# Two more feed-forward tiles beside the attention, and the last unit's reciprocals spread over rows by the matmul engine

## The chip, the cores and the metric

The kernel runs on one core of a Trainium2 chip. The metric is the device time of one execution in microseconds (us). Engines are named as in the profile: PE (matmul), DVE (vector), ACT (scalar), POOL (GpSimd), SP (sync, which issues most transfers).

## The reference

One transformer block with modulation, for 2048 tokens of width 512 in fp32 (F is 1792):

```
mod = silu(c) @ w_mod                            # six vectors of 512: sa, ca, ga, sb, cb, gb
h = layernorm(x) * (1 + ca) + sa
q, k, v = h @ wqkv                               # 32 heads of 16
x = x + ga * (softmax(q k^T / 4) v) @ wo
h = layernorm(x) * (1 + cb) + sb
x = x + gb * ((silu(h @ w_gate) * (h @ w_up)) @ w_down)
```

## The kernel before

**Layout.** The 2048 queries are cut into four chunks of 512 (`NC`, `CW`). Four heads of one chunk are a **unit**; there are 8 x 4 = 32 units (`NU`), and each has 16 **steps**, one for each 128 keys, so 512 steps (`n`) in all. A step is four **pairs**, one for each head. A pair (`pair_of`, L961) is a score matmul (L568) with its exponential on ACT (L570), and beside it on other rows of the array a matmul (L521) that finds, 20 steps ahead, the maxima of a later unit, reduced by DVE (L523). After step 491 no maxima are left. The product with V (`pv_step`, L574, matmuls at L583) follows at least two steps behind. The exponentials are L570, four to a step (one of 128 x 512 for each head), so the number of L570 instructions up to a moment, divided by four, is the step that has been reached.

**Sums of the softmax.** V carries a column of ones, so row 16 of each head's 32 rows in the result `o` is the sum of its exponentials. When a unit ends, `out_a` to `out_c` (L590 to L611) move the four sums (4 x 512 numbers) to a 128 x 16 tile `dn`, take reciprocals (L598), store them to DRAM (L599), load them again with every head's row repeated 32 times (L604), multiply (L610) and store the result to DRAM (`o_dr`, L611). `load_o` (L721) gathers it from there, 16 of each 32 rows, for the output projection; `split_o` (L726) splits it into a high and a low part (L729, L730).

**Precision.** Most products are three matmuls of split operands (high x high, high x low, low x high) in a single-pass format; the array takes fp32 operands in several records.

**Filler.** While units of chunk 1 to 3 run, the output projection and feed-forward of the chunk before stand between their pairs. `plain(steps)` (L1018) runs steps without filler; `filled(places, work)` (L1032) runs two steps (eight pairs) and takes after each pair as many items of `work` as the table `TWO`, `DOWN` or, once no maxima are left, `ALONE` (L50 to L52) says. Filler matmuls use 64 rows of the array at a time (L781), two banks (`FBANKS`, 3 and 6). One gate-and-up tile (`gate_up`, 128 of the 1792 columns) fills four steps; a down job fills two. The 28 jobs of a chunk are in `Chunk.jobs` (L694).

**The order around the change.** For chunk 2, whose feed-forward stands beside the last units: plain to step 403, the projection to step 411, 9 plain steps (`NORM`), 3 with transposes, then `REST` = 24 plain steps to step 447, then all jobs but the last `KEEP` = 7 to step 511, and one step without filler (L1080). The seven jobs left (gate-up tiles 11 and 12, the two downs of pair 5, tile 13, the two downs of pair 6) are run by `whole` (L1086) after the attention with matmuls of 128 rows (L791).

**The end.** After the last product with V (L1101), PE runs in program order: 36 projection matmuls of the last chunk for k = 0 to 2 (`out_terms`, L824), 48 matmuls of tiles 11 and 12 (L1114), 12 projection matmuls for k = 3, which need the last unit's output, then 48 matmuls of the downs and tile 13 (L1123), the transposes of the new rows (L765) and the last chunk's feed-forward. Meanwhile `out_b`, `out_r`, `out_c`, `load_o` and `split_o` of the last unit are issued from ACT (L1109 to L1113).

Of the kernel before, what the change touches and what calls it, by code (L numbers as in the profile page):

```python
# [9 lines left out]
F32 = mybir.dt.float32  # L10
# [9 lines left out]
P = 128  # L20
# [3 lines left out]
DH = 16  # L24
F = 1792
NT = S // P
NK = D // P
NC = 4
CW = S // NC
NG = H // 4  # L30
NU = NG * NC
# [11 lines left out]
UG = 16 * NG  # L43
PTS = 13
FBANKS = (3, 6)
KEEP = 7
REST = 24
NORM = 9
STARTS = (147, 275, 403)
TWO = (0, 3, 2, 2, 2, 2, 1, 0)  # L50
# [4 lines left out]
def run(it):  # L55
    for _ in it:
        pass


def take(it, k):  # L60
    run(islice(it, k))
# [40 lines left out]
def block_kernel(ctx, tc, x, wqkv, wo, w_gate, w_up, w_down, c, w_mod, out):  # L102
    nc = tc.nc
# [8 lines left out]
    banks = [ps.tile([P, CW], F32, name=f"bank{i}") for i in range(8)]  # L112
# [11 lines left out]
    ident = const.tile([P, P], F32, name="ident")  # L124
# [11 lines left out]
    o_dr = dram.tile([NC, NG, P, CW], F32, name="o_dr")  # L136
# [355 lines left out]
    pf = None  # L492
    qop, mx, pts, pv, o_, due, res = {}, {}, {}, {}, {}, {}, {}
    posts = []
    n = 16 * NU
    last = NC - 1
# [75 lines left out]
    def pv_step(i, half):  # L572

        u, kt = divmod(i, 16)  # L574
        g = u % NG
        cols = slice(half * HQ, (half + 1) * HQ)
        if kt == 0 and half == 0:
            pv[u] = single("pv")
            o_[u] = pf.tile([P, CW], F32, name="o", tag="o", bufs=2)
        p_ = pts.pop(i) if half else pts[i]  # L580
        for h in range(4):
            e0 = (kt * H + 4 * g + h) * (DH + 1)
            nc.tensor.matmul(pv[u][32 * h:32 * h + 32, cols], v_flat[:, e0:e0 + 32], p_[h][:, cols],  # L583
                             start=(kt == 0 and half == 0), stop=(kt == 15),
                             skip_group_check=half == 1)
        if kt == 15 and half:
            nc.scalar.copy(o_[u], pv[u])
# [9 lines left out]
    def out_b(u, eng, o, dn):  # L597
        nc.vector.reciprocal(dn, dn)  # L598
        eng.dma_start(d_dr[u].rearrange("h (b e) -> (h b) e", e=16), dn)  # L599
        return o,  # L600

    def out_r(u, eng, o):
        rb = pf.tile([P, CW], F32, name="rb", tag="rb", bufs=1)
        eng.dma_start(rb, d_dr[u][:, None, :].to_broadcast([4, 32, CW]))  # L604
        return o, rb

    def out_c(u, eng, mul, o, rb):
        ci, g = divmod(u, NG)
        on = pf.tile([P, CW], F32, name="on", tag="on", bufs=1)
        mul.tensor_mul(on, o, rb)  # L610
        eng.dma_start(o_dr[ci, g], on)  # L611

    def at(i, f):
        due.setdefault(i, []).append(f)
# [16 lines left out]
    def tmp(name):  # L631
        return pf.tile([P, CW], F32, name=name, tag="tmp", bufs=4)
# [56 lines left out]
    class Chunk:  # L689
# [31 lines left out]
        def load_o(self, eng, ks=range(NK)):  # L721
            for k in ks:
                src = o_dr[self.ci, 2 * k:2 * k + 2].rearrange("g (h e) s -> (g h) e s", e=32)[:, 0:DH, :]
                eng.dma_start(self.oT[1][:, k, :].bitcast(F32), src)

        def split_o(self, ks=range(NK), alone=False):  # L726
            for k in ks:
                hi, lo = self.oT[0][:, k, :], self.oT[1][:, k, :]
                (nc.scalar.copy if alone else nc.gpsimd.tensor_copy)(hi, lo.bitcast(F32))  # L729
                (nc.vector if alone else nc.gpsimd).tensor_sub(lo, lo.bitcast(F32), hi.bitcast(F32))  # L730
# [90 lines left out]
    def out_terms(ch, t, pt, ks):  # L821
        for k in ks:
            for a, b in ((0, 0), (0, 1), (1, 0)):
                nc.tensor.matmul(pt, ch.oT[a][:, k, t * P:(t + 1) * P], ch.wo[k // 2][:, b, k % 2, :],  # L824
                                 start=(k == 0 and a == b == 0), stop=(k == NK - 1 and a == 1))
# [46 lines left out]
    chunks = {}  # L872
# [21 lines left out]
    def hook():  # L894
        while posts:
            posts.pop(0)()
# [64 lines left out]
    def pair_of():  # L961
        nonlocal done
        i = done // 4 - 1
        most = 4 * n - 4 * (LEAD - 1)
        h = (ORDER if done < most else (0, 1, 2, 3))[done % 4]
        work = [lambda: score(i + 1, h)]
        if done < most:
            work.insert(1 - h % 2, lambda: max_one(done + 4 * (LEAD - 1)))
        for f in work:
            f()  # L970
        done += 1
        if side:
            side.pop(0)()
# [22 lines left out]
    def pvs(most, by_halves):  # L996

        nonlocal owed
        if by_halves:
            most, owed = most + owed, 0  # L1000
        while most and halves and 4 * halves[0][0] + 8 <= done:
            i, half = halves.pop(0)
            pv_step(i, half)
            most -= 1
            if i % 16 == 15 and half:
                close_unit(i // 16, done // 4 - 1)
                if by_halves:
                    break
        if by_halves and most and halves and 4 * halves[0][0] + 8 <= done:
            owed = most  # L1010

    def end_steps():
        nonlocal ended
        while ended < done // 4:
            after(ended - 1)
            ended += 1

    def plain(steps, tails=()):  # L1018

        nonlocal four, bank, beside  # L1020
        beside = False
        assert steps % WIN == 0 and done % 4 == 0
        four, bank = Turn(0, 1, 2, 3), Turn(4, 5, 6)
        for w in range(4 * steps // WIN):
            for _ in range(WIN):
                pair_of()
            if w >= 4 * steps // WIN - len(tails):
                tails[w - 4 * steps // WIN](four())
            pvs((HALVES[(w - 2) % 4] if done > 8 else 0) + (w == 4 * steps // WIN - 1), True)
            end_steps()  # L1030

    def filled(places, work):  # L1032

        nonlocal four, bank, beside
        beside = True
        four, bank = three, Turn(4, 5)
        if done >= 4 * n - 4 * (LEAD - 1):
            places, bank = ALONE.get(places, places), Turn(4, 5, 0, 1, 2)
        for r in range(len(places)):
            pair_of()  # L1040
            take(work, places[r])
            if r % 4 == 3:
                end_steps()
        hook()
        pvs(6, False)
# [9 lines left out]
    at(n - 24, begin_last)  # L1055
    at(n - 13, lambda: chunks[last].load_o(nc.gpsimd, range(NK - 1)))
    at(n - 11, lambda: chunks[last].split_o(range(NK - 1)))
    outs = [banks[b] for b in FBANKS]
    pvs(3, False)
    for ci in range(last):  # L1060
        plain(STARTS[ci] - done // 4)
        ch = chunks[ci]
# [7 lines left out]
        if ci == last - 1:  # L1070
            plain(REST)
        for _ in range(len(ch.jobs) - (KEEP if ci == last - 1 else 0)):
            job, args = ch.jobs.pop(0)
# [3 lines left out]
            for places in (TWO, TWO) if job is gate_up else (DOWN,):  # L1077
                filled(places, work)
    chunks[last - 1].load_gu(NF - 2)
    filled((0,) * 4, iter(()))  # L1080


    assert done == 4 * n
    turns = chain([2, 3, 2, 0, 1, 2, 0], cycle([1, 3, 2, 0]))

    def whole(ch, jobs):  # L1086
        for job, args in jobs[:-2]:
            b = 2 * next(turns)
            for _ in job(ch, *args, banks[b:b + 2], False):
                yield  # L1090
            hook()
        both = []
        for job, args in jobs[-2:]:
            b = 2 * next(turns)
            both.append(job(ch, *args, banks[b:b + 2], False))
        for g in both * 2:
            yield from islice(g, 6)
            hook()

    for i, half in halves:  # L1100
        pv_step(i, half)  # L1101
    after(n - 1)
    close_unit(NU - 1, n)
    ch, chp = chunks[last], chunks[last - 1]
    rest = whole(chp, chp.jobs)
    ch.load_x2(nc.gpsimd)
    for t in range(4):
        out_terms(ch, t, banks[t], range(NK - 1))
    on = out_b(NU - 1, nc.scalar, *res[NU - 1])  # L1109
    on = out_r(NU - 1, nc.scalar, *on)  # L1110
    out_c(NU - 1, nc.scalar, nc.vector, *on)
    ch.load_o(nc.scalar, (NK - 1,))
    ch.split_o((NK - 1,), True)  # L1113
    take(rest, 48)  # L1114
    for t in range(4):
        out_terms(ch, t, banks[t], (NK - 1,))
        if t % 2:
# [41 lines left out]
```

## Time and profile before

| what | value |
|---|---|
| median of 3 runs | 1838.07 us (1837.73 to 1839.37) |
| the profiled execution | 1838.88 us |
| its span, first to last instruction | 1837.1 us |
| PE busy | 1825.5 us, 99% of the span |
| DVE, ACT, POOL busy | 1532.5, 1243.7, 460.4 us |
| granted PE clock | 1.00 throughout |

Each row of a timeline gives a start, a duration, the engine, the line, the operation, what it writes and reads, and in brackets how long the engine had been idle and what ended that. A row of windows gives, for a stretch of the span, each engine's busy time and in parentheses how many instructions reach into it. "SPq", "ACTq" and "POOLq" are instructions that only issue a transfer. PE matmuls overlap: a matmul of 512 columns is shown as about 0.39 us and the next one starts some 0.23 us after it, so a PE that is shown as busy may still be waiting a little.

### The profile page before, as it was taken

What the parts mean: (1) busy time and instruction counts of PE and PEld (TensorE: products, weight loads), DVE (VectorE), ACT (ScalarE), POOL (GpSimd) and SP (SyncE); (2) the same over time, 40 slices, a digit from 0 to 9 for tenths busy, and PEclk for the clock granted to TensorE, in tenths of its full rate; (3) what the DMA queues carried; (4) which work ended last, traced back from release to release, by engine and by line L of the source; (5) the groups of instructions that cost most, each with busy time, mean ns of one, the idle gap of its engine ahead of it and who ended that gap; (6) DMA issues with size and microseconds to landing.
All of it is one profiled execution on the core that took longest, in us unless ns stands there. A gap on an engine that the chain in (4) does not pass through costs nothing.

```text
span 1837.1 us, 41048 instructions
## 1 busy us (share of the span) xinstructions
PE 1825.5 (99%) x16904; PEld 1198.2 (65%) x16904; DVE 1532.5 (83%) x2578; ACT 1243.7 (68%) x2386; POOL 460.4 (25%) x541
## 2 busy tenths in 40 slices
PE   9999999999999999999999999999999999999999
PEld 7876444444455777776565777776564577777887
DVE  5578999999999888889999888889999988831544
ACT  4223888888877777777878777777878877774211
POOL 3612544565223111111123111111123011130200
PEclk9999999999999999999999999999999999999999
DMA  8884876657845444453544554444643545333642
GB/s 305 286 225 149 183 185 199 168 189 178 209 79 125 102 120 141 118 147 70 149 103 105 134 132 116 123 117 90 158 81 57 111 93 149 138 122 121 271 169 110
DMA packets 80488, 267.63 MB, mean 146 GB/s; under 512 B 19604, under 2 KB 24212, under 8 KB 59620
## 3 DMA queue, kind: packets, MB, share of 16 engines
q1 hardware_dynamic: 61324, 179.71, 33.8%
q0 software_dynamic: 18288, 84.49, 19.3%
q8 instruction: 133, 2.18, 0.5%
q10 hardware_dynamic: 688, 0.80, 0.2%
q14 instruction: 55, 0.45, 0.1%
HBM read 201.85 MB, written 62.13 MB: 144 GB/s over the span
## 4 chain that ended last, share of the span: by engine, by line
PE 96%; DVE 2%; ACT 1%; DMA 1%; SPq 0%; issue 0%; DVEq 0%
PE bank L583 27%; PE bank L781 19%; PE bank L568 18%; PE bank L521 14%; PE bank L791 8%; PE bank L211 7%; DVE mx L523 1%; PE bank L824 1%; DMA wm_ab<-in_w_mod 1%; PE bank L765 0%; DVE stt L807 0%; PE bank L533 0%; PE bank L163 0%; PE bank L534 0%; PE bank L535 0%
## 5 line engine op out<-in xcount | busy, mean ns | idle before, releaser
L523 DVE TENSOR_REDUCE mx<-bank 128x1 f32<-128x512 f32 x2048 | 1276.0, 681 | 108.5 <-PE bank L521 66.2
L568 PE MATMUL bank<-qop,kop 50*128 50x512 f32 x2048 | 730.2, 425 | 1.0 <-ACT pt__16517 L570 0.2
L521 PE MATMUL bank<-kop,qop 48*128 48x512 f32 x2048 | 726.6, 425 | 2.9 <-DVE mx L523 2.6
L568 PEld LDWEIGHTS bank<-qop,kop 50*128 50x128 f32 x2048 | 342.6, 184 | 169.9 <-issue 55.6
L521 PEld LDWEIGHTS bank<-kop,qop 48*128 48x128 f32 x2048 | 343.5, 184 | 113.9 <-DVE mx L523 67.7
L781 PE MATMUL bank<-act,wgu 64*128 64x512 f32 x1872 | 300.9, 392 | 0.0
L781 PEld LDWEIGHTS bank<-act,wgu 64*128 64x128 f32 x1872 | 196.1, 187 | 24.7 <-issue 0.2
L610 POOL TENSOR_TENSOR on<-o,rb 128x512 f32<-128x512 f32 x31 | 39.8, 1284 | 498.1 <-DMA rb<-d_dr 363.6
L781 PE MATMUL bank<-wd,mid 64*128 64x512 f32 x912 | 134.0, 397 | 0.0
L843 POOL CAST mid<-m 128x512 fp32r<-128x512 f32 x40 | 24.3, 608 | 379.3 <-DVE m L841 176.5
L781 PEld LDWEIGHTS bank<-wd,mid 64*128 64x128 f32 x912 | 88.0, 185 | 15.9 <-ACT first L878 3.2
L211 PE MATMUL bank<-hT,wqs 128*128 128x512 f32 x384 | 94.3, 397 | 0.4 <-DVE wqs L351 0.4
L839 DVE SCALAR_TENSOR_TENSOR q<-th,bank 128x512 f32<-128x512 f32 x56 | 38.2, 682 | 54.4 <-ACT th L835 54.4
L211 PEld LDWEIGHTS bank<-hT,wqs 128*128 128x128 f32 x384 | 70.7, 188 | 18.8 <-issue 2.9
L835 ACT ACTIVATE th<-bank 128x512 f32<-128x512 f32 x56 | 33.3, 594 | 58.1 <-PE bank L791 58.1
L855 DVE TENSOR_TENSOR x<-bank,x 128x512 f32<-128x512 f32 x84 | 53.9, 685 | 18.3 <-PE bank L781 16.8
L841 DVE TENSOR_TENSOR m<-bank,q 128x512 f32<-128x512 f32 x56 | 38.7, 691 | 21.7 <-PE bank L791 19.7
L844 POOL TENSOR_TENSOR mid<-m,mid 128x512 fp32r<-128x512 f32 x40 | 51.5, 1287 | 3.3
L791 PE MATMUL bank<-wd,mid 128*128 128x512 f32 x216 | 51.4, 393 | 0.0
L211 PE MATMUL bank<-wqs,hT 128*128 128x512 f32 x192 | 48.0, 398 | 0.0
L781 PE MATMUL bank<-wgu,act 64*128 64x512 f32 x288 | 47.8, 394 | 0.1
L791 PEld LDWEIGHTS bank<-wd,mid 128*128 128x128 f32 x216 | 40.3, 188 | 9.1 <-POOL mid L844 0.3
(6298 smaller groups left out, 5133.0 us busy)
## 6 DMA issues: line engine op xcount, KB each, us to landing
wgu<-gu_dr SPq DMA_DIRECT2D x48, 1024.0 KB
wd<-wd_dr SPq DMA_DIRECT2D x28, 1024.0 KB
kop<-kd SPq DMA_DIRECT2D x33, 768.0 KB
kop<-kd POOLq DMA_DIRECT2D x29, 768.0 KB, 8.8
gu_dr<-wgu POOLq DMA_DIRECT2D x14, 1024.0 KB, 13.5
kd<-prt SPq DMA_DIRECT2D x16, 512.0 KB
qd<-prt SPq DMA_DIRECT2D x16, 512.0 KB
kop<-gu_dr SPq DMA_DIRECT2D x8, 1024.0 KB
```

Of the source, the lines that this page charges most:

```text
L211: nc.tensor.matmul(pt, lhs(a, k), rhs(b, k), start=(n == 0), stop=(n == 3 * nk - 1))
L521: nc.tensor.matmul(pm, qop[u][rows, s, qt * P:(qt + 1) * P], kop[u % 3][rows, s, kc * CW:(kc + 1) * CW], start=True, stop=True)
L523: nc.vector.tensor_reduce(mx[u][:, b, s, qt, kc:kc + 1], pm, op=ALU.max, axis=AX.X)
L568: nc.tensor.matmul(sp, kop[u % 3][rows, h // 2, kt * P:(kt + 1) * P], qop[u][rows, h // 2, :], start=True, stop=True)
L583: nc.tensor.matmul(pv[u][32 * h:32 * h + 32, cols], v_flat[:, e0:e0 + 32], p_[h][:, cols], start=(kt == 0 and half == 0), stop=(kt == 15), ...
L610: mul.tensor_mul(on, o, rb)
L781: nc.tensor.matmul(outs[e], lhs(e, a, k)[rows], rhs(b, k)[rows], start=(ph == 0 and j == 0), stop=(j == z and (ph == 1 or trade is not None)),
L791: nc.tensor.matmul(outs[e], lhs(e, a, k), rhs(b, k), start=(j == 0), stop=(j == z))
L839: nc.vector.scalar_tensor_tensor(q, th, 1.0, outs[0], op0=ALU.add, op1=ALU.mult)
L841: nc.vector.tensor_mul(m32, outs[1], q)
L844: (nc.gpsimd if slow else nc.vector).tensor_sub(mid[:, 1, :], m32, mid[:, 0, :].bitcast(F32))
L855: nc.vector.tensor_add(ch.x2[:, t, :], outs[e], ch.x2[:, t, :])
```

## The change

- `KEEP` goes from 7 to 5 and `REST` from 24 to 15: tiles 11 and 12 move from behind the attention to its steps 502 to 509; the jobs begin at step 438 instead of 447, and nine plain steps go. The steps without filler at the end become two.
- The two projection loops at the end are cut: 18 matmuls (t = 0, 1) before and 18 (t = 2, 3) behind a new fp32 matmul, and the 48 matmuls of tiles 11 and 12 are no longer there.
- The last unit's reciprocals no longer go through DRAM. DVE multiplies the 128 x 16 reciprocals by a pattern `eye` (one where the row's number within its head is the block's number) into a 128 x 512 tile `spread`; one PE matmul with a block matrix of ones (`block`) sums the 32 rows of each head, so that all 32 rows hold the head's 512 reciprocals, in bank 6; DVE multiplies `o` by it. POOL builds `block` and `eye` beforehand with eight small instructions.
- The last unit's output no longer goes through DRAM. Four transfers within SBUF (two from ACT, two from SP, 16 rows of 2 KB each) bring it to the projection's operand. The half of k = 3 that belongs to the unit before is loaded on POOL by `load_half`, due after step 506.

```diff
--- before.py
+++ after.py
@@ -43,8 +43,8 @@
 UG = 16 * NG
 PTS = 13
 FBANKS = (3, 6)
-KEEP = 7
-REST = 24
+KEEP = 5
+REST = 15
 NORM = 9
 STARTS = (147, 275, 403)
 TWO = (0, 3, 2, 2, 2, 2, 1, 0)
@@ -723,6 +723,10 @@
                 src = o_dr[self.ci, 2 * k:2 * k + 2].rearrange("g (h e) s -> (g h) e s", e=32)[:, 0:DH, :]
                 eng.dma_start(self.oT[1][:, k, :].bitcast(F32), src)
 
+        def load_half(self):
+            src = o_dr[self.ci, NG - 2].rearrange("(h e) s -> h e s", e=32)[:, 0:DH, :]
+            nc.gpsimd.dma_start(self.oT[1][0:4 * DH, NK - 1, :].bitcast(F32), src)
+
         def split_o(self, ks=range(NK), alone=False):
             for k in ks:
                 hi, lo = self.oT[0][:, k, :], self.oT[1][:, k, :]
@@ -1055,6 +1059,7 @@
     at(n - 24, begin_last)
     at(n - 13, lambda: chunks[last].load_o(nc.gpsimd, range(NK - 1)))
     at(n - 11, lambda: chunks[last].split_o(range(NK - 1)))
+    at(n - 6, lambda: chunks[last].load_half())
     outs = [banks[b] for b in FBANKS]
     pvs(3, False)
     for ci in range(last):
@@ -1077,11 +1082,11 @@
             for places in (TWO, TWO) if job is gate_up else (DOWN,):
                 filled(places, work)
     chunks[last - 1].load_gu(NF - 2)
-    filled((0,) * 4, iter(()))
+    filled((0,) * 8, iter(()))
 
 
     assert done == 4 * n
-    turns = chain([2, 3, 2, 0, 1, 2, 0], cycle([1, 3, 2, 0]))
+    turns = chain([2, 0, 1, 2, 0], cycle([1, 3, 2, 0]))
 
     def whole(ch, jobs):
         for job, args in jobs[:-2]:
@@ -1097,6 +1102,14 @@
             yield from islice(g, 6)
             hook()
 
+    place = tmp("place")
+    block, eye = place[:, 0:P], place[:, P:P + 32]
+    nc.gpsimd.memset(block, 0.0)
+    for h in range(4):
+        nc.gpsimd.memset(block[32 * h:32 * h + 32, 32 * h:32 * h + 32], 1.0)
+    nc.gpsimd.tensor_add(eye, ident[:, 0:32], ident[:, 32:64])
+    for h in (2, 3):
+        nc.gpsimd.tensor_add(eye, eye, ident[:, 32 * h:32 * h + 32])
     for i, half in halves:
         pv_step(i, half)
     after(n - 1)
@@ -1104,14 +1117,22 @@
     ch, chp = chunks[last], chunks[last - 1]
     rest = whole(chp, chp.jobs)
     ch.load_x2(nc.gpsimd)
-    for t in range(4):
+    for t in range(2):
         out_terms(ch, t, banks[t], range(NK - 1))
-    on = out_b(NU - 1, nc.scalar, *res[NU - 1])
-    on = out_r(NU - 1, nc.scalar, *on)
-    out_c(NU - 1, nc.scalar, nc.vector, *on)
-    ch.load_o(nc.scalar, (NK - 1,))
+    o, dn = res.pop(NU - 1)
+    nc.vector.reciprocal(dn, dn)
+    spread = tmp("spread")
+    nc.vector.tensor_mul(spread.rearrange("p (b e) -> p b e", e=16), dn[:, None, :].to_broadcast([P, 32, 16]),
+                         eye[:, :, None].to_broadcast([P, 32, 16]))
+    nc.tensor.matmul(banks[6], block, spread, start=True, stop=True)
+    on = pf.tile([P, CW], F32, name="on", tag="on", bufs=1)
+    nc.vector.tensor_mul(on, o, banks[6])
+    for h in range(4):
+        (nc.sync if h % 2 else nc.scalar).dma_start(
+            ch.oT[1][(4 + h) * DH:(5 + h) * DH, NK - 1, :].bitcast(F32), on[32 * h:32 * h + DH, :])
     ch.split_o((NK - 1,), True)
-    take(rest, 48)
+    for t in range(2, 4):
+        out_terms(ch, t, banks[t], range(NK - 1))
     for t in range(4):
         out_terms(ch, t, banks[t], (NK - 1,))
         if t % 2:
```

On PE, at the end of the loop over steps. Names are the program's: `bank_63` to `bank_70` are banks 0 to 7, L568 is a score, L583 a product with V. Before, the four scores of step 511 stand without filler:

```order
L568 MATMUL bank_67<-qop,kop_971 128x512
L568 MATMUL bank_68<-qop,kop_971 128x512
L568 MATMUL bank_63<-qop,kop_971 128x512
L568 MATMUL bank_64<-qop,kop_971 128x512
L583 MATMUL bank_70<-pt__20656,v_flat 32x256
L583 MATMUL bank_70<-pt__20659,v_flat 32x256
L583 MATMUL bank_70<-pt__20678,v_flat 32x256
```

After, the eight scores of steps 510 and 511:

```order
L568 MATMUL bank_67<-qop,kop_971 128x512
L568 MATMUL bank_68<-qop,kop_971 128x512
L568 MATMUL bank_63<-qop,kop_971 128x512
L568 MATMUL bank_64<-qop,kop_971 128x512
L568 MATMUL bank_65<-qop,kop_971 128x512
L568 MATMUL bank_67<-qop,kop_971 128x512
L568 MATMUL bank_68<-qop,kop_971 128x512
L568 MATMUL bank_63<-qop,kop_971 128x512
L583 MATMUL bank_70<-pt__20759,v_flat 32x256
L583 MATMUL bank_70<-pt__20762,v_flat 32x256
L583 MATMUL bank_70<-pt__20775,v_flat 32x256
```

One more step's scores stand in a row without filler; the three products with V that follow (of steps 509 to 511) are two before.

On PE, behind the last product with V. Before (the L791 rows go on to 48 matmuls of tiles 11 and 12, and then come the four L824 rows x3 for k = 3):

```order
L824 MATMUL bank_63<-kop_1509,kop_88 128x512 x9
L824 MATMUL bank_64<-kop_1509,kop_88 128x512 x9
L824 MATMUL bank_65<-kop_1509,kop_88 128x512 x9
L824 MATMUL bank_66<-kop_1509,kop_88 128x512 x9
L791 MATMUL bank_67<-act_16126,wgu 128x512
L791 MATMUL bank_67<-act_16127,wgu 128x512
L791 MATMUL bank_67<-act_16126,wgu 128x512 x2
L791 MATMUL bank_67<-act_16127,wgu 128x512
```

After (the projection is L828 in the changed kernel, the new matmul L1127, the downs L795):

```order
L828 MATMUL bank_63<-kop_1509,kop_88 128x512 x9
L828 MATMUL bank_64<-kop_1509,kop_88 128x512 x9
L1127 MATMUL bank_69<-spread,place 128x512
L828 MATMUL bank_65<-kop_1509,kop_88 128x512 x9
L828 MATMUL bank_66<-kop_1509,kop_88 128x512 x9
L828 MATMUL bank_63<-kop_1509,kop_88 128x512 x3
L828 MATMUL bank_64<-kop_1509,kop_88 128x512 x3
L828 MATMUL bank_65<-kop_1509,kop_88 128x512 x3
L828 MATMUL bank_66<-kop_1509,kop_88 128x512 x3
L795 MATMUL bank_67<-wd,mid 128x512 x6
```

The new matmul stands between the two halves of the projection for k = 0 to 2, and the k = 3 rows follow the second half at once.

On ACT, from the copy of the last unit's result out of its bank to the split of the last projection operand (`kop_88` is that operand, `th` belongs to a feed-forward tile). Before:

```order
L587 COPY o<-bank_70 128x512
L594 DMA dn<-o 128x1x16
L599 DMA d_dr<-dn 128x16
L604 DMA rb<-d_dr 128x1x512
L611 DMA o_dr<-on 128x512
L724 DMA kop_88<-o_dr 128x1x512
L729 CAST kop_88<-kop_88 128x512
L835 ACTIVATE th<-bank_67 128x512
```

After:

```order
L587 COPY o<-bank_70 128x512
L594 DMA dn<-o 128x1x16
L1131 DMA kop_88<-on 16x512 x2
L733 CAST kop_88<-kop_88 128x512
L761 ACTIVATE v_flat<-v_flat,rs_20920,rs 128x512 x2
L839 ACTIVATE th<-bank_65 128x512
```

The two trips to DRAM and back (L599 with L604, L611 with L724) are gone from ACT's queue, and two of the four new transfers stand in their place; the other two are on SP.

## The prediction

> **What bounds the kernel now.** The page first: its busy line, and the chain that ended last.
>
> ```profile
> PE 1825.5 (99%) x16904; PEld 1198.2 (65%) x16904; DVE 1532.5 (83%) x2578; ACT 1243.7 (68%) x2386; POOL 460.4 (25%) x541
> PE 96%; DVE 2%; ACT 1%; DMA 1%; SPq 0%; issue 0%; DVEq 0%
> ```
>
> PE is on the chain for 96% of the span. So the change is worth what it takes from PE's program, less what it adds there and the waits that it makes. But busy PE has two rates beside the attention, so the second view is the windows of L570 alone (the exponentials: their count over four is the step). An exponential that began just before a stretch is counted with it, so a count is up to two high.
>
> ```profile
> 0.00:1440.92 1440.92, 950.39 (x1753) 1.00 0.57 146
> 1440.92:1463.89 22.97, 18.81 (x38) 1.00 0.21 71
> 1463.89:1470.98 7.09, 4.57 (x9) 1.00 0.88 232
> 1470.98:1579.58 108.60, 73.22 (x129) 1.00 0.47 120
> 1579.58:1620.11 40.53, 27.33 (x49) 1.00 0.40 145
> 1620.11:1672.76 52.65, 38.53 (x72) 1.00 0.36 114
> ```
>
> These are steps 0 to 437; 438 to 446 (nine plain steps, those that go); 447 and 448 (the first filled ones); 449 to 480; 481 to 492; and 493 to 510 (18 steps with filler and no maxima). A plain step takes 22.97 / 9 = 2.55 us, a filled one 108.60 / 32 = 3.394, one without maxima 52.65 / 18 = 2.925. Whose limit each is, two rows of the groups tell: DVE's maxima in the nine plain steps, then in steps 449 to 480.
>
> ```profile
> L523 DVE TENSOR_REDUCE mx<-bank 128x1 f32<-128x512 f32 x38 | 23.1, 677 | 0.3 <-PE bank L521 0.2
> ...
> L523 DVE TENSOR_REDUCE mx<-bank 128x1 f32<-128x512 f32 x129 | 82.9, 685 | 13.9 <-PE bank L521 9.1 <-PE bank L568 3.9
> ```
>
> In plain steps DVE reduces without a break and PE has room; in filled ones DVE waits 13.9 us for PE. So filler beside the attention is cheap, not free: 3.394 - 2.55 = 0.84 us a step, some 3.4 us for a tile of four steps, against what it costs alone. That is in the last view, the chain in order of time behind the last steps:
>
> ```profile
> 1669.97 0.23 PE bank L781 x2
> ...
> 1672.96 2.97 PE bank L583 x32
> 1675.93 8.60 PE bank L824 x36
> 1684.53 10.89 PE bank L791 x48
> 1695.42 2.99 PE bank L824 x12
> 1698.41 10.99 PE bank L791 x48
> ```
>
> The last filler ends at 1670.20. From 1672.96 on the pieces touch: PE hardly waits here. The trips through DRAM that the change cuts short are covered by the 48 matmuls of tiles 11 and 12, so a shorter chain alone earns nothing; it only makes it possible to take these 48 away. They cost 10.89 us, 5.45 a tile.
>
> **Part 1: the loop over steps.** Before, step 438 to the start of step 493 takes 22.97 + 7.09 + 108.60 + 40.53 = 179.19 us. After, steps 438 to 491 are filled with maxima: 54 steps, of which the first two cost 7.09 as they do now and 52 cost 3.394 each, 176.49. What the end of a plain stretch loses moves with it and stays. The last two plain steps show that loss:
>
> ```profile
> 1457.61:1463.89 6.28, 6.28 (x72) 3.06 (x69) 6.02 (x10) 4.71 (x11) 0.00 (x0) 1.00 0.49 168
> ```
>
> The other seven take (22.97 - 6.28) / 7 = 2.38, so these two are 1.51 over. A part belongs to this unit's row of maxima, which went through PE here, and goes; a part is the extra product with V and the turn to filler, and stays. Between 0 and 1.51 I take the middle, 0.8. Sum: 0.8 + 7.09 + 176.49 - 179.19 = **+5.2 us**. The 18 steps without maxima stay 18.
>
> The second step without filler at the end is new. PE has few matmuls there, so ACT sets the pace:
>
> ```profile
> 1672.76 0.60 ACT L570 ACTIVATE pt__20702<-bank 128x512 f32<-128x512 f32 x1 [1.21 <-PE bank L568]
> 1673.26 0.59 ACT L570 ACTIVATE pt__20705<-bank 128x512 f32<-128x512 f32 x1
> ...
> 1674.21 0.62 ACT L570 ACTIVATE pt__20711<-bank 128x512 f32<-128x512 f32 x1
> 1675.97 0.59 ACT L587 COPY o<-bank 128x512 f32<-128x512 f32 x1 [1.14 <-PE bank L583]
> 1676.59 1.12 ACTq L594 DMA_DIRECT2D dn<-o  x1
> 1678.89 0.35 ACTq L599 DMA_DIRECT2D d_dr<-dn  x1
> 1681.13 0.56 ACTq L604 DMA_DIRECT2D rb<-d_dr  x1
> 1687.01 0.32 ACTq L611 DMA_DIRECT2D o_dr<-on  x1
> 1689.14 0.61 ACTq L724 DMA_DIRECT2D kop<-o_dr  x1
> 1694.41 0.62 ACT L729 CAST kop<-kop 128x512 fp32r<-128x512 f32 x1 [17.85 <-DMA kop<-o_dr]
> ```
>
> Three exponentials start within 1.45 us, 0.483 each; four more make **+1.9 us**. They lie ahead of the last product with V, which needs the last of them.
>
> **Part 2: behind the last product with V.** Call its end T (1675.93 now). Before, 8.60 + 10.89 = 19.49 us pass from T to the k = 3 projection. After, PE has 18 matmuls (8.60 / 2 = 4.30), the new fp32 one, and 18 more (4.30). The nearest row for the new one is L314, of the same shape and type, between rows of L211:
>
> ```profile
> 85.62 1.29 PE L211 MATMUL bank<-wqs,hT 128*128 128x512 f32 x5
> 86.75 1.02 PE L314 MATMUL bank<-wm,one 128*128 128x512 f32 x2
> 87.21 2.18 PE L211 MATMUL bank<-wqs,hT 128*128 128x512 f32 x7
> ```
>
> From 85.62 to 89.39 stand twelve L211 and this one (two records). Twelve alone, 10.89 / 48 = 0.227 apart and 0.39 long at the end, take 2.89; so it costs 0.88. Without waits: 4.30 + 0.88 + 4.30 = 9.48, that is **-10.0 us**.
>
> Would PE wait? The chain after T, by the ACT rows above and these of DVE (the SPq row is a load of 1024 KB for tile 13):
>
> ```profile
> 1678.60 0.26 DVE L598 RECIPROCAL dn<-dn 128x16 f32<-128x16 f32 x1 [7.00 <-DMA dn<-o]
> 1686.28 0.69 DVE L610 TENSOR_TENSOR on<-o,rb 128x512 f32<-128x512 f32 x1 [7.42 <-DMA rb<-d_dr]
> ...
> 1690.00 0.32 SPq L714 DMA_DIRECT2D wgu<-gu_dr  x1
> ...
> 1695.06 0.69 DVE L730 TENSOR_TENSOR kop<-kop 128x512 fp32r<-128x512 f32 x1 [8.09 <-ACT kop L729]
> ```
>
> Copy, transfer of `dn` and reciprocal end at T + 2.93 (1678.86), in a stretch in which the transfer engines were nearly idle (share 0.14):
>
> ```profile
> 1676.60:1678.60 2.00, 2.00 (x10) 1.59 (x10) 0.00 (x0) 0.00 (x0) 0.00 (x0) 1.00 0.14 37
> ```
>
>  The spread multiply writes 128 x 512 like L610: T + 3.7 (it may cost 0.26, the reciprocal's, to twice 0.69; even then 4.4). PE comes to the matmul at T + 4.30, so 0.6 us of delay in `dn` are free. They may be needed: the 1024 KB load of `x2`, long landed now, will be in flight then (below). The slowest transfer beside such a load is L724's, over L714's at 1690.00: 1694.41 - 1689.14 = 5.27 for 256 KB; `dn` at 2.01 means no wait, at 5.27 a wait of 2.7. `dn` has a 32nd of that size, so I stay near 2.01 and add **0.3**. Without that, the result stands 1.02 later; the multiply by bank 6 ends at T + 6.1. Then two transfers each on ACT and SP. Issuing takes 0.32 to 1.12 on ACT; I take 0.45. From issue to use, `dn` (8 KB, within SBUF) took 1678.60 - 1676.59 = 2.01, `o_dr` (256 KB) 1689.14 - 1687.01 = 2.13, `rb` (256 KB from DRAM) 1686.28 - 1681.13 = 5.15. Ends 2.0 and 5.15; I take 2.1, since 32 KB lie between the first two. Landed at T + 8.65, cast (0.62) done at T + 9.3, against T + 9.48 when PE asks: the low half, 0.69 later, is asked for two matmuls later too: 0.1 more, so **+0.4 us** of waits; at 5.15 a transfer they would be 3.5, with an issue of 1.12 they would be 1.1.
>
> The rest lies under cover. POOL builds `block` and `eye` behind tile 12's split and ahead of the load of `x2`. The split of the tile before, and rows for what a small operation on POOL costs:
>
> ```profile
> 1657.99 0.40 PE L781 MATMUL bank<-act,wgu 64*128 64x512 f32 x2
> ...
> 1657.92 1.28 POOL L610 TENSOR_TENSOR on<-o,rb 128x512 f32<-128x512 f32 x1 [6.88 <-DMA rb<-d_dr]
> 1661.40 1.29 POOL L844 TENSOR_TENSOR mid<-m,mid 128x512 fp32r<-128x512 f32 x1
> ...
> 0.73 0.20 POOL masks.py:197 MEMSET ident<- 128x128 f32 x1 [0.29 <-POOLq L1148]
> ```
>
> That split ended 1662.69 - 1658.39 = 4.3 us after its tile's last matmul. Tile 12's last matmul takes the place of the filler's end, 1675.93 - 1670.20 = 5.7 us ahead of T, and 1.9 more with the added step: T - 7.6, so its split ends at T - 3.3. Eight operations cost between 0.20 (128 x 128 memset) and 1.28 (128 x 512 product) each. At 0.3, near the first since all are small, they end at T - 0.9, 5 us early, and the load of `x2` is issued then; at 1.28 at T + 6.9, and PE waits 2.6. `load_half` is issued on POOL after step 506; what queues behind its wait, tile 12's split, isn't asked for until the downs behind the attention. On DVE the three operations of tile 11 that stood ahead of the residual adds are gone, so the norm of the last chunk comes earlier against PE, not later. ACT's cast queues behind its two transfers, in the chain already.
>
> **Sum:** +5.2 + 1.9 - 10.0 + 0.4 = **-2.5 us**. The profiled execution took 1838.88, so 1836.4 there; it lies 0.8 above the median of the runs, so against that 1838.07 - 2.5 = **1835.6**.
>
> **A rule of the Trainium skill that speaks against the four transfers.** The trace has the small `dn` transfer at 2.01 us, alone. "DMA: Bandwidth & Descriptors" (Rules for kernel authors) says of two transfers to disjoint partition halves that they serialize, and advises one transfer. If the four overlap but for their issue, as I took it, the sum stays -2.5; by the rule taken at its word they follow one another, and the sum is that of the second rival, which is priced from rows. No run here shows four like these.
>
> **Rivals.** *The filler is cheaper than I take it*: nothing is lost at the plain stretch's end (-0.8), and the first two filled steps, now 7.09 where a unit also closes, cost 2 x 3.394 (-0.3). Then -3.6, 1834.5; with no wait for `dn` (-0.3) it is 1834.2. For it: both extras are seen only once. Against: the turn from plain to filled is in the program either way. If half of the added step is hidden too (PE has matmuls of its own there), another 1.0 goes: 1833.2.
>
> *Slower: the four transfers come one after the other.* The mechanism's place is between the multiply by bank 6 (T + 6.1) and the cast. Four in a row at 2.1 land at T + 14.5, the cast is done at T + 15.1, PE waits 5.6 instead of 0.1 and the sum is +3.0: 1841.1. At `rb`'s 5.15 with two on each queue in a row they land at T + 16.4: wait 7.5, +4.9, 1843.0. It decides from a wait of 2.6 us on. For it: L724's 5.27 beside another load. Against: that load was 32 times as large as one of the four, and here nothing large is left in flight by then.
>
> *The chain is late without that*: `dn` or one of the four near 5.2, or the POOL pattern late. PE waits 1.5 to 3.5 us, the sum lies between -1.4 and +0.6: 1836.7 to 1838.7. So the change then does what it says and PE stands idle instead of working on tiles 11 and 12.
>
> **How the numbers follow.** A measurement of this kernel can tell about 0.2% (3.7 us) from no change. Forecast 0.50 (its own range 1834.5 to 1836.7), cheaper filler 0.27, late chain 0.16, transfers in a row 0.07. The first and third lie within 0.2%, the second beyond it on the fast side; the fourth counts as slower, though its lower price is still within. The range reaches from 1833.2 to 1838.7 and leaves out the slow rival and the tails.
>
> **What would show it.** In the profile after: L570 counts that put step 438 near 1441 and the start of step 492 near 1625; filled steps of 3.39; two last steps with exponentials 0.48 apart; behind the last L583, 18 matmuls, one L1127 of two records, 18, then 12 with less than 0.5 us between; L733's cast starting about 8.7 us after the end of L583. A gap before the k = 3 rows, ended by a transfer, speaks for the late rivals; a first cast at T + 14 for the slow one. Step times other than 3.39 would make Part 1 wrong, and any wait ahead of the transposes that is not there now would make my cover claims wrong.

## The result, and the profile after

| | before | after |
|---|---|---|
| median of 14 runs each | 1839.03 us (1837.72 to 1840.53) | 1841.49 us (1840.43 to 1843.42) |
| ratio | 1 | 1.0018 [1.0011, 1.0025] |
| span of the profiled execution | 1837.1 us | 1839.2 us |
| last product with V ends (T) | 1675.93 | 1686.34 |
| from T to the end of the span | 161.16 us | 152.88 us |

The change makes the kernel 2.5 us slower (0.18%). Forecast was 2.5 us faster. The spans differ by +2.1 us: +10.4 up to T, -8.3 behind it. The page after, its busy line and its chain:

```profile
PE 1823.1 (99%) x16948; PEld 1199.6 (65%) x16948; DVE 1535.1 (83%) x2580; ACT 1244.1 (68%) x2384; POOL 463.7 (25%) x552
PE 94%; DVE 3%; ACT 2%; DMA 1%; issue 0%; SPq 0%; ACTq 0%; DVEq 0%
```

PE is busy for 2.4 us less than before in a span that is 2.1 us longer, and its share of the chain falls from 96% to 94%: PE has begun to wait. The windows of L570 say where (stretch, its length, ACT's busy time and count, then the granted clock, the busy share of the transfer engines and GB/s). The stretches are steps 0 to 437; 438 to 449 (the first six filled calls of two steps); 450 to 481; 482 to 491 (the last steps with maxima); 492 to 509 (filler, no maxima); and 510 to T. Each stretch begins where a call begins, so the calls stay whole.

```profile
0.00:1441.39 1441.39, 950.30 (x1753) 1.00 0.57 146
1441.39:1482.91 41.52, 27.75 (x49) 1.00 0.30 109
1482.91:1593.50 110.59, 72.93 (x128) 1.00 0.48 123
1593.50:1627.48 33.98, 22.72 (x40) 1.00 0.47 159
1627.48:1681.20 53.72, 38.81 (x72) 1.00 0.34 115
1681.20:1686.34 5.14, 4.03 (x8) 1.00 0.02 3
```

The working of the forecast, put on these stretches, gives 41.03 (7.09 and ten steps of 3.394), 108.61, 33.94, 52.65 and 5.07 (3.17 and the 1.9 of the added step). Measured less forecast: +0.49, +1.98, +0.04, +1.07, +0.07, which is 3.65 us. The excess is not spread over the steps. Steps 482 to 491 hold no unit's end and came out as forecast. The other filled stretches hold four ends: one, two, and (in the last) one. The waits of PE and of PEld (its loading of weights) at the products with V name what happens there (in us: total, times, longest). Before:

```profile
PEld bank L583 <- ACT o L587: 5.1, 17, 0.4
```

After:

```profile
PEld bank L583 <- ACT o L587: 10.2, 21, 1.5
PE bank L583 <- ACT o L587: 3.1, 4, 1.0
```

PE now stands idle four times, 3.1 us in all, for ACT's copy of a unit's result out of its bank, and before it never did. The timeline of the first of the four (PE and ACT; first and last product of each half of the block):

```profile
1479.54 0.40 PE L583 MATMUL bank<-pt__18140,v_flat 128*32 128x256 f32 x1
...
1480.23 0.38 PE L583 MATMUL bank<-pt__18167,v_flat 128*32 128x256 f32 x1
1480.68 0.58 ACT L587 COPY o<-bank 128x512 f32<-128x512 f32 x1
1481.32 0.40 PE L583 MATMUL bank<-pt__18186,v_flat 128*32 128x256 f32 x1 [0.70 <-ACT o L587]
...
1482.01 0.38 PE L583 MATMUL bank<-pt__18213,v_flat 128*32 128x256 f32 x1
```

One block of products with V holds the last step of a unit (447) and the first of the next (448). Both go to bank 7. The second half can't begin before the copy (1480.68 to 1481.26) has emptied it. The block's starts reach from 1479.54 to 1482.01, 2.47 us, where a block of as many products within one unit takes 1.56. Over the four blocks (2.47, 2.47, 2.47, 2.77) that is 3.9 us.

Behind T, the chain in order of time (start, duration, what):

```profile
1683.33 3.02 PE bank L583 x48
...
1686.37 0.60 ACT o L587
...
1686.99 3.31 DMA dn<-o
...
1690.40 0.26 DVE dn L1123
...
1690.76 0.70 DVE spread L1125
...
1691.50 1.14 PE bank L1127 x2
...
1692.72 0.70 DVE on L1129
...
1694.08 2.30 DMA kop<-on
...
1696.52 0.63 ACT kop L733
...
1697.19 3.33 PE bank L828 x12
1700.52 2.52 PE bank L795 x11
```

Where before only PE stood here, the chain now runs through the new operations one after another: `dn`, reciprocal, spread, matmul, multiply, transfers, cast. The k = 3 projection starts at T + 10.85 where T + 9.9 was forecast (9.48 and the 0.4 of waits), and its 12 matmuls take 3.33 us where I had 2.99, since the low half (DVE, 0.69 behind the cast) comes while they run. Together 1.3 us, most of it by `dn`: 1686.99 to 1690.40 is 3.41 us, where 2.01 was taken. The timeline shows what PE lost by it, and what was in flight: POOL's load of `x2` (into `v_flat`), in the listing of transfers with its size and the time to its landing.

```profile
1684.66 0.82 POOL L703 DMA_DIRECT2D v_flat<-in_A_x  x1
...
1691.50 1.13 PE L1127 MATMUL bank<-spread,place 128*128 128x512 f32 x2 [0.77 <-DVE spread L1125]
```

```profile
v_flat<-in_A_x POOLq DMA_DIRECT2D x1, 1024.0 KB, 5.9
```

Issued 2.33 us ahead of `dn`, the load lands at 1684.66 + 5.9 = 1690.56, and `dn` with it.

### The profile page after: what moved, and what is told of

Its sections match the earlier page's. It is cut to its first block, busy times and chain, and to the rows that moved or that the text cites. A ratio compares the mean times of both kernels' runs of the same rounds, so it can differ in the third digit from the quotient of the medians.

```text
span 1839.2 us, 41174 instructions
## 1 busy us (share of the span) xinstructions
PE 1823.1 (99%) x16948; PEld 1199.6 (65%) x16948; DVE 1535.1 (83%) x2580; ACT 1244.1 (68%) x2384; POOL 463.7 (25%) x552
## 4 chain that ended last, share of the span: by engine, by line
PE 94%; DVE 3%; ACT 2%; DMA 1%; issue 0%; SPq 0%; ACTq 0%; DVEq 0%
PE bank L583 26%; PE bank L785 20%; PE bank L568 18%; PE bank L521 14%; PE bank L211 7%; PE bank L795 7%; DVE mx L523 2%; PE bank L769 0%; DMA wm_ab<-in_w_mod 0%; DVE stt L811 0%; PE bank L533 0%; PE bank L163 0%; PE bank L828 0%; DMA dn<-o 0%; PE bank L535 0%
## 5 line engine op out<-in xcount | busy, mean ns | idle before, releaser
L568 PE MATMUL bank<-qop,kop 50*128 50x512 f32 x2048 | 732.3, 426 | 1.4 <-ACT pt__20803 L570 0.2
L568 PEld LDWEIGHTS bank<-qop,kop 50*128 50x128 f32 x2048 | 343.8, 185 | 170.2 <-issue 56.7
L785 PE MATMUL bank<-act,wgu 64*128 64x512 f32 x1968 | 315.0, 392 | 0.0
L785 PEld LDWEIGHTS bank<-act,wgu 64*128 64x128 f32 x1968 | 204.9, 187 | 26.1 <-issue 0.2
L211 PE MATMUL bank<-hT,wqs 128*128 128x512 f32 x384 | 94.2, 397 | 0.4 <-DVE wqs L351 0.4
L211 PEld LDWEIGHTS bank<-hT,wqs 128*128 128x128 f32 x384 | 70.7, 188 | 18.6 <-issue 3.0
L795 PE MATMUL bank<-wd,mid 128*128 128x512 f32 x216 | 51.3, 393 | 0.0
L211 PE MATMUL bank<-wqs,hT 128*128 128x512 f32 x192 | 48.0, 398 | 0.0
L795 PEld LDWEIGHTS bank<-wd,mid 128*128 128x128 f32 x216 | 40.5, 188 | 8.8
```

The source lines that it names most:

```text
L211: nc.tensor.matmul(pt, lhs(a, k), rhs(b, k), start=(n == 0), stop=(n == 3 * nk - 1))
L568: nc.tensor.matmul(sp, kop[u % 3][rows, h // 2, kt * P:(kt + 1) * P], qop[u][rows, h // 2, :], start=True, stop=True)
L785: nc.tensor.matmul(outs[e], lhs(e, a, k)[rows], rhs(b, k)[rows], start=(ph == 0 and j == 0), stop=(j == z and (ph == 1 or trade is not None)),
L795: nc.tensor.matmul(outs[e], lhs(e, a, k), rhs(b, k), start=(j == 0), stop=(j == z))
```

## The experiments

Theory: the loss has two causes. *Parity*: `REST` = 15 makes the filled calls of two steps begin on even steps, so that a unit's end falls inside a block of products with V. *x2*: the load of `x2` delays `dn`. Rivals: filled steps are dearer than 3.394 wherever they stand; the new end is slow in itself (its four transfers, its chain). The first four kernels shared 33 runs of the kernel before (median 1838.82), the last four 21 (1838.52).

**One unfilled step ahead of the jobs** (`odd_start`), the changed kernel with the calls on odd steps again:

```diff
             plain(REST)
+            filled((0,) * 4, iter(()))
...
-    filled((0,) * 8, iter(()))
+    filled((0,) * 4, iter(()))
```

> The changed kernel with one of its two unfilled steps moved ahead of the jobs, so that the filled two-step calls start on odd steps (439) as they did before the change. Theory (a call that starts on an even step runs the product with V of a unit's last step and of the next unit's first step in one block, in one bank, and PE waits there for ACT's copy): the four long steps (449, 465, 481, 497, about 5.1 us against 4.2) shorten to 4.2, some 3.6 us go, an unfilled step with maxima costs 0.5 to 0.7 more than one without; so 0.5 us faster than the kernel before (between 1.5 faster and 0.5 slower). Rival (filled steps here are dearer for another reason, as loads or DVE): the long steps stay or move, time 2.5 to 3.2 us above the kernel before.

1841.41 us, ratio 1.0013 [1.0004, 1.0022], 2.6 above the kernel before where 0.5 below was expected. In the loop it did what parity says. Waits, then windows (the 32 filled steps from 449, the next 12, the 18 without maxima):

```profile
PEld bank L583 <- ACT o L587: 5.1, 17, 0.4
```

```profile
1478.29:1587.09 108.80, 72.89 (x129) 1.00 0.45 119
1587.09:1627.63 40.54, 27.34 (x48) 1.00 0.40 143
1627.63:1680.11 52.48, 38.85 (x72) 1.00 0.34 111
```

These are the 108.60, 40.53 and 52.65 of before again, and T comes at 1683.28, 3.06 earlier than after. So the filled step costs 3.39 as forecast, and the first rival falls. But the gain was lost behind T, in one row of the chain:

```profile
1683.93 5.55 DMA dn<-o
```

With one unfilled step less at the end, the load of `x2` was issued at 1683.57, 0.36 us ahead of `dn` instead of 2.33. It landed at 1689.47, and `dn` was used at 1689.57, 5.64 us after its issue. PE waited 3.0 us for the spread. My expectation held for the loop and missed this collision, which the second cause should have told me.

**The block broken at a unit's end** (`held_pv`): even calls as after, but the next unit's first products wait until two pairs into the next call.

```diff
             if i % 16 == 15 and half:
                 close_unit(i // 16, done // 4 - 1)
-                if by_halves:
-                    break
+                if not by_halves:
+                    held = most
+                break
...
             take(work, places[r])
+            if r == 1 and held:
+                most, held = held, 0
+                pvs(most, False)
```

> The changed kernel with its even start, but at a unit's end the block of products with V stops, and the new unit's first step follows two pairs into the next filled call. Steps and transfers stay where they are. Theory (PE waits for the copy out of bank 7 between the two): the gap before L583 at the four unit ends goes, 3 to 3.6 us less than the changed kernel, that is about 0.9 us faster than the kernel before (0 to 1.5 faster). Rival (the even start costs something else): within 0.5 us of the changed kernel, 2.0 to 3.0 us above the kernel before.

1841.71 us, 1.0018 [1.0009, 1.0027]: a miss, and the number is the rival's. The wait is gone (17 times, 5.1 us, no row of PE), and yet from step 438 to step 511 this execution takes 242.69 us where after takes 241.74. (Its T lies 2.2 us behind after's; 1.24 of that was there at step 438 already.) Each of the four unit ends still costs 0.9 to 1.4 us against before. So taking away the wait isn't enough, if the products are cut into two smaller blocks; what exactly the second block costs stays open. Its rows show 0.1 us at each turn into and out of a block, and at three of the four ends a step of 0.63 to 0.70 us between two filler matmuls where 0.23 is usual (the first at 1483.09, ended by DVE), which is not all. Whether the wait for the bank is by itself the price of an even start is therefore not shown; that an even start has this price is.

**`x2` loaded earlier** (`early_x2`), on POOL after step 504 of the program in place of behind the loop (issued at 1657.31 instead of 1684.66):

```diff
+    at(n - 8, lambda: chunks[last].load_x2(nc.gpsimd))
...
-    ch.load_x2(nc.gpsimd)
```

> The changed kernel with the 1024 KB load of x2 issued some ten steps earlier on POOL. Theory (the small transfer of dn took 3.4 us instead of 2.0 because it shares the engines with that load): dn takes 2.0 to 2.1 again, PE does not wait at the spread matmul (0.8 now), 1.0 to 1.4 us less than the changed kernel, so 1.2 us above the kernel before (0.8 to 1.8). Rival (it is the issue from ACT or the order of the queue): dn stays at 3.4 and the time 2.5 us above the kernel before.

1840.17 us, 1.0009 [1.0000, 1.0018]; against after's +2.5 it is +1.35. Its chain behind T = 1686.36:

```profile
1686.36 4.39 PE bank L828 x18
1690.75 0.87 PE bank L1127 x2
...
1693.06 2.30 DMA kop<-on
...
1696.17 3.33 PE bank L828 x12
```

From its issue to the reciprocal `dn` takes 2.04 us, as ACT's and DVE's rows show:

```profile
1687.01 1.15 ACTq L594 DMA_DIRECT2D dn<-o  x1
```

```profile
1689.05 0.25 DVE L1123 RECIPROCAL dn<-dn 128x16 f32<-128x16 f32 x1 [8.14 <-DMA dn<-o]
```

PE passes from the 18 matmuls to L1127 without a gap. The k = 3 rows start at T + 9.81 and not T + 10.85: 1.04 us was the load's. The matmuls take 4.39 + 0.87 + 4.19 = 9.45 of it, so 0.36 is left as a wait for the cast. The new end isn't slow in itself.

**The new end alone** (`tail_alone`): the kernel before, `KEEP` and `REST` unchanged, with the new end in front of the 48 matmuls of tiles 11 and 12.

```diff
-    on = out_b(NU - 1, nc.scalar, *res[NU - 1])
...
+    nc.tensor.matmul(banks[6], block, spread, start=True, stop=True)
...
     take(rest, 48)
```

> The kernel before with the new end alone: reciprocals spread by PE, output moved within SBUF, half loaded early, but tiles 11 and 12 left behind the attention in their place ahead of the k = 3 projection. Theory (PE did not wait for the trips through DRAM, so a shorter chain alone earns nothing): 0.9 us slower than the kernel before, the spread matmul's price (0.4 to 1.5). Rival (the chain's end, or ACT and DVE on it, did hold PE up): 1 us faster or more.

1839.31 us, 1.0003 [0.9994, 1.0012]. The cast of `kop` starts on ACT at 1685.11, and its reader at 1696.30, behind the cover:

```profile
1685.40 10.89 PE bank L795 x48
1696.30 2.79 PE bank L828 x12
```

The time is within noise of the kernel before, and a chain 9 us shorter is worth nothing while 10.89 us of other work stand over it.

**Both repairs** (`odd_early`): the edits of `odd_start` and `early_x2` together.

> The changed kernel with both repairs: the jobs start on an odd step (one unfilled step ahead of them, one at the end) and x2 is loaded some ten steps earlier. Theory (the change's loss is the waits at unit ends, some 3.6 us, and dn's transfer behind the load of x2, 1 to 2.5 us): the loop as in the odd start alone (last product with V 7.4 us after that of the kernel before), the end as in the early x2 alone (9.3 us less from there), so 2.0 us faster than the kernel before (1.4 to 2.6). Rival (each repair uncovers the other's loss, or the end depends on the unfilled step): not faster than the kernel before.

1836.97 us, 0.9993 [0.9984, 1.0001], 1.55 below before (spans -2.1). T is 1683.13 and the rest 151.84 us: the loop of the first repair and the end of the second, each as it was alone. The two causes add, and the span comes near the -2.5 that was forecast, though the interval still touches no change.

**And four matmuls moved under the last wait** (`odd_early_cover`):

```diff
     for t in range(2, 4):
         out_terms(ch, t, banks[t], range(NK - 1))
+    take(rest, 4)
...
-    take(rest, 48)
+    take(rest, 44)
```

> As the kernel with both repairs, and four matmuls of the next down taken ahead of the k = 3 projection, where PE waits 0.4 us for the cast and 0.3 us for the low half. Theory (the end's chain is only some 0.7 us too long): these waits go, 2.6 us faster than the kernel before (1.9 to 3.2). Rival (the wait moves to another place behind): the same as with both repairs alone, 2.0 us faster.

1836.39 us, 0.9988 [0.9979, 0.9996]: 2.1 us faster than the kernel before, and the lowest time here. The 0.6 us between it and both repairs alone is less than either interval is wide; the traces agree with a gain (spans 1833.7 and 1835.0). The pieces on PE touch:

```profile
1687.14 0.86 PE bank L1128 x2
1687.99 4.19 PE bank L828 x18
1692.18 0.92 PE bank L795 x4
1693.10 2.86 PE bank L828 x12
1695.96 10.03 PE bank L795 x44
```

The 12 matmuls of k = 3 now take 2.86 us, not 3.33, since the low half is there when they ask for it.

**The kernel before on even steps** (`before_even`): the converse of `odd_start`, its one unfilled step moved ahead of the jobs.

```diff
             plain(REST)
+            filled((0,) * 4, iter(()))
...
-    filled((0,) * 4, iter(()))
```

> The kernel before, all its own parts, but with its unfilled step ahead of the jobs instead of behind them, so that the filled calls start on even steps (448). Theory (even starts make PE wait at each unit's end): four waits of 0.9 us appear at steps 449, 465, 481 and 497, and the time is 3.8 us above the kernel before (3.0 to 4.5). Rival (the even start costs nothing of itself; the changed kernel lost by its added jobs): 0 to 0.5 us above it.

1844.38 us, 1.0037 [1.0024, 1.0049], 5.9 above and so outside the expected range. The four waits appear in a kernel that has nothing else of the change:

```profile
PEld bank L583 <- ACT o L587: 9.9, 21, 1.2
PE bank L583 <- ACT o L587: 2.9, 4, 0.8
```

T comes 4.1 us later than before; 0.6 of that was there at step 438, so the four ends cost 3.5. The other 2.0 lie behind T and I had not expected them: without the unfilled step at the end, transfers collide again, `dn` at 3.57 and `kop` at 6.64 us, and the 48 matmuls no longer cover the trip through DRAM. This time it is SP's two loads of 1024 KB (issued at 1677.15 and just behind) that are in flight with `dn`.

```profile
1680.76 3.57 DMA dn<-o
...
1693.91 6.64 DMA kop<-o_dr
```

**The jobs without the new end** (`jobs_alone`): the changed kernel's `KEEP`, `REST` and loop, with the end of before and so no tiles 11 and 12 over it.

```diff
-    nc.tensor.matmul(banks[6], block, spread, start=True, stop=True)
...
+    on = out_b(NU - 1, nc.scalar, *res[NU - 1])
+    on = out_r(NU - 1, nc.scalar, *on)
+    out_c(NU - 1, nc.scalar, nc.vector, *on)
+    ch.load_o(nc.scalar, (NK - 1,))
```

> The changed kernel's loop (KEEP 5, REST 15, two unfilled steps) with the end of the kernel before, its trips through DRAM included; only tiles 11 and 12 are no longer there to cover them. Theory (the moved jobs cost 10.6 us in the loop as in the changed kernel, and the trip through DRAM then leaves PE idle until about 18 us after the last product with V): 9 us above the kernel before (7.5 to 10.5). Rival (the trips were longer than needed because of tile 13's load, and without that nearly fit under the 36 matmuls): 3 us above or less.

1849.39 us, 1.0058 [1.0044, 1.0072]. The old trip, laid bare, takes until T + 17.2, and the 12 matmuls behind it are themselves slow. Windows (stretch, its length, busy us and counts of PE, PEld, DVE, ACT and POOL, the granted clock, the transfer engines' share, GB/s), and the row of the chain:

```profile
1694.00:1702.40 8.40, 0.00 (x0) 0.00 (x0) 0.69 (x1) 0.62 (x1) 0.00 (x0) 0.74 0.20 64
1702.40:1708.00 5.60, 5.57 (x13) 4.36 (x14) 3.91 (x8) 0.00 (x0) 0.00 (x0) 0.50 0.01 3
1708.00:1712.00 4.00, 4.00 (x18) 3.23 (x18) 3.66 (x14) 0.00 (x0) 0.00 (x0) 0.96 0.00 0
```

```profile
1702.43 5.49 PE bank L828 x12
```

After 8.4 us in which PE did nothing, it works at a clock of 0.50. Against the 3.33 us of the other kernels with a wait there, 2.2 us are lost, about the excess over what I had expected. The two parts of the change need each other: the jobs alone are +10.9 us, the end alone about +0.5, and both +2.5.

## Why the prediction was wrong, point by point

- **What bounds the kernel**: right. PE's program sets the time, and nearly every difference found is a change in it or a wait of it (the exception is its clock, below).
- **Part 1, +5.2: wrong, +8.7 measured** (step 438 to the end of the steps without maxima, and the turn ahead of it). The step that failed is "52 cost 3.394 each": the rate was read from calls that begin on odd steps and used for calls that begin on even ones. At 3.394 no unit's end lies inside a block. Four blocks came to hold one, 0.9 to 1.2 us each. `odd_start` and `before_even` show it in both directions. The working counted the products with V, but did not ask which unit two neighbours in a block belong to, though they are written to one bank that ACT must empty in between. (`held_pv` takes that wait away and gains nothing, so the price of the even start is shown, and its make-up only in part.) The rest of Part 1 held: the turn to filler cost 0.7 (step 438 moves from 0.23 ahead of before to 0.47 behind), where I took 0.8, and apart from the waits the filled steps were 0.4 cheaper.
- **The added unfilled step, +1.9**: right, 5.14 - 3.17 = 1.97.
- **Part 2, -10.0 on PE**: right. 18 matmuls take 4.39 and 4.19 us (4.30 each), the fp32 matmul 0.87 (0.88), wherever nothing made PE wait. The price from L314 between rows of L211 held.
- **The waits, +0.4: wrong, 1.7 measured**: 1.04 for `dn` (I took 0.3), 0.36 for the cast (none), 0.34 for the low half (0.1). "I stay near 2.01 and add 0.3" failed: size was taken as the measure of what a small transfer suffers beside a large one, and it landed with the large one. A row to warn of it was there: the listing of transfers before has 6.1 us from the issue of this load to its landing. I issued it at T - 0.9 and never wrote down that it lands at T + 5.2, where I wanted `dn` at T + 2.93.
- **POOL's pattern**: right. The eight operations took 0.14 to 0.29 each and were done 1.6 us ahead of T (0.9 forecast).
- **The four transfers**: right. 2.93 us from the first issue to the last landing (1693.44 to 1696.37), of which 0.6 is the issue of the second. They overlap. Their packets ran side by side (1694.69 to 1695.72 on one queue, 1694.82 to 1696.02 on the other). The slow rival, and with it the rule of the Trainium skill that was weighed ("DMA: Bandwidth & Descriptors", Rules for kernel authors), would have given some 8.4; no row here bears that out for 32 KB each on two queues.
- **The rivals**: the late chain was half right, in its cause (`dn`) and not in its size. Slower by waits inside the loop was in none of them. The line on what would show it did point there: step times other than 3.39. It was a check on the number, when it should have been a mechanism with a price.
- **Sum**: forecast -2.5; +3.55 in the loop, +1.3 at the end, and 0.2 less from what lies ahead of step 438 make +2.1, the difference of the spans. (This execution is 0.6 ahead of before's at step 411 and loses 0.4 of that by step 420, in 3.4 us at half the clock.)

## What to carry to other kernels

A rate that is read from a loop holds only for the same phase of it: when the change moves where calls begin, look at which instructions become neighbours, and whether they share a bank that another engine has to empty first. Try the other phase before taking the wait apart: here moving one step ahead of the calls gave most of the loss in the loop back, and splitting the block did not. A small transfer on the critical path should not be issued while a large one is on its way, on whatever queue: put the large load early, or behind it. When covering work is taken away, give each trip that becomes visible its own line in the sum, with everything that is in flight at that moment.

## What the hardware did that I had not expected

- **A transfer of 8 KB waits for the 1024 KB load issued ahead of it on another queue.** `dn` took 2.04 us with nothing large in flight, 3.41 with the load issued 2.33 us ahead, and 5.64 with it issued 0.36 us ahead; in the last two it landed within 0.3 us of the load. In `before_even`, behind SP's loads, it took 3.57 and landed at 1684.33, 0.14 behind the last of their packets. The Trainium skill ("DMA: Bandwidth & Descriptors", Queues, rings and completion order) says that a transfer's semaphore increment lands only after every earlier write of the same transfer engine, across its queues. The landings agree with that, but it is not all: the 128 packets of `dn` themselves began 1.31 us after the issue in `early_x2`, 2.38 in the changed kernel and 4.11 in `odd_start`, only when the load's packets were about to end (1690.10 and 1688.98). So the data was held back too, and not only its increment; the runs don't show by what.
- **The clock of PE after an idle stretch.** In `jobs_alone` it was 0.74 on the mean of 8.4 idle us (1.00 in the first 4.2, then 0.50) and 0.50 in the 5.6 us after them, and back at 1.00 from 1708.3. Behind T of the other kernels, with waits of at most 3.0 us, it stayed at 1.00. "TensorE: Matmul & The Clock Gate" (Part 1) of the Trainium skill has a halved clock after about 3.4 us without work and full speed after as long a busy time; the runs agree with the first, and saw some 5.9 us of work (1702.43 to about 1708.3) before the clock was back. The loop holds something that this rule doesn't account for: the clock was 0.50 for 3.4 us without any such idle stretch ahead, once in the execution of the changed kernel (from 1373.2; PE was busy for 3.35 of the 3.40 us before), three times in that of `held_pv` and twice in that of `before_even`. The one in the changed kernel cost the 0.4 us above. Why some executions have it stays open.
- **Issuing a transfer on ACT is not cheap**: 0.59 and 0.61 us for the two L1131, where I took 0.45, and 1.14 for `dn`.
